# Attention's buffers handed to the experts' weights in seven parts instead of five, and one piece of output multiplied later

## The chip, the cores and the metric

The kernel runs on one core of one Trainium2 chip. The metric is the device time of one execution in microseconds (us). A core has five instruction streams that matter here: PE (TensorE, matrix products), DVE (VectorE), ACT (ScalarE), POOL (GpSimd) and SP (SyncE). SP computes nothing: it issues the transfers (DMA) between the device's memory and the on-chip memory, one after another, in the order of the program.

## The reference, cut to what matters

Attention over hashed buckets for 4 batches of 8 heads (768 positions, 64 wide), and behind it a soft mixture of 8 experts with 4 slots each.

```python
# attention, for each of the 32 (batch, head)
q_bucket = bits of (q @ proj > 0);  k_bucket likewise          # 6 bits
scores = where(q_bucket == k_bucket, (q @ k.T) / 8, -1e9)
out    = softmax(scores) @ v
x = out arranged as (3072 tokens, 512)
# soft mixture of experts
logits = x @ phi                                    # 32 slots
slot_input = softmax(logits, over tokens).T @ x     # 8 experts x 4 slots
slot_out[e] = relu(slot_input[e] @ w1[e]) @ w2[e]   # w1: 512x1024, w2: 1024x512, 8 experts
return softmax(logits, over slots) @ slot_out       # (3072, 512)
```

All numbers are 32-bit floats. The experts' weights are 32 MB and are read once.

## The kernel before, in words

**Attention.** The 32 heads run one behind another, two at a time in flight. For each head the kernel loads q and k, hashes and splits them, and puts them into one of three buffers `XY` (head h uses XY[h % 3]). PE then makes each head's scores twice: once for the maximum of each row (`smax`), and once for the exponentials (`scores`, line 711, which also needs one row of `XY` that is written late by a small transfer, `shift_rows`, line 576). ACT takes the exponentials into one of five buffers `pt` (line 717), POOL adds them up into one of three `acc` (lines 725 and 728), and PE multiplies them with v (`av`, line 737). v is loaded by `load_v` (line 558) into one of two buffers, head h into v[h % 2].

The order of the work is written out by hand: `at` (line 1050) takes each step with a time from the tables `WHEN`, `FIRST` and `LAST`, the steps are sorted by that time, and the loop that begins at line 1128 goes through whole-numbered slots and calls the steps of each slot in order. Six slots belong to a head, and `last` is slot 192, where the last head would begin to end. What a step emits goes to the queues of its engines in that order, so SP's queue has the loads and moves in the order in which the steps were called. SP waits at each transfer until the place that it writes is free and until the transfer eight before it in its own queue has landed, and everything behind it waits too.

**Weights.** The weights are cut into 64 pieces of 512 KB, tiles `w` of 128 x 1024, loaded in the order in which they will be used by `load_weights` (line 449) and `load_piece` (line 454; line 457 for w1, line 459 for w2). 22 pieces have buffers of their own (pool `wa`) and come in during attention, one every six slots. For the rest there is no room while attention runs. Attention's own buffers lie in pools on the other side of the memory, stacked upon one another, and are closed from the top as attention ends; pools of weights are opened in their place:

- slot `last` - 14: `pp` (raw q and k, their splits, the bits) becomes `wb`, 5 pieces, of which one is loaded in each of five slots
- slot `last` - 5: `yp` (two of the three `XY`) becomes `wy`, 6 pieces
- slot `last` - 2: `ap` (three of the five `pt`, two of the three `acc`, one of the two v) becomes `wp`, 6 pieces
- slot `last`: `lp` (one `pt`, one `XY`) becomes `wl`, 5 pieces
- slot `last` + 2: `mp` (the last `pt`, the last `acc`, the other v and small things) becomes `wc`, 1 piece

The other 19 pieces go into buffers that are used a second time: three into the last batch's tokens (`xq`), 16 into `wa`'s once their first pieces have been multiplied.

**Experts and output.** PE multiplies the slots with w1 (`hidden`, line 1191) and the result with w2 (`model`, line 1245), the second in two halves x of 256 columns each. `split_out` (line 1249) splits a half's result in two parts that are multiplied together later: ACT copies it (line 1251), DVE makes the rest (line 1252). `send` (line 1256) then makes the output of a half in six pieces: for each piece PE makes two products of two matmuls each (line 1266), DVE copies the one and ACT the other into a tile `w` of 512 KB (line 1268), and SP sends the tile out (line 1269). The tiles for sending, and one more, `halves`, for the split parts, come from `wy`'s six buffers. The end of the program is: the first half's `model`; `split_out`; 16 matmuls of the second half's `model`; `send` of the first half, six pieces; the other 48 matmuls of the second half's `model`; `split_out`; `send` of the second half, six pieces.

Of the kernel before, what the change touches and what calls it, by code (L numbers as in the profile page):

```python
# [9 lines left out]
F32 = mybir.dt.float32  # L10
F32R = mybir.dt.float32r
# [5 lines left out]
B, H, S, D, NB = 4, 8, 768, 64, 6  # L17
BH = B * H
P = 128
NT = S // P  # L20
# [3 lines left out]
E, SPE, F = 8, 4, 1024  # L24
# [8 lines left out]
N_R = 2 * NB + 1  # L33
N_Y = 3
N_P = 5
N_WA, N_WB, N_WY, N_WP, N_WL, N_WC = 22, 5, 6, 6, 5, 1


C_TH, C_AM, C_LO = 0, 1, 2
# [369 lines left out]
def held_pool(tc, name):  # L409
    stack = ExitStack()  # L410
    return stack.enter_context(tc.tile_pool(name=name, bufs=1, side="right")), stack.close
# [3 lines left out]
def lsh_attention_soft_moe(  # L415
# [15 lines left out]
    wa = ctx.enter_context(tc.tile_pool(name="wa", bufs=N_WA))  # L431
    dp = ctx.enter_context(tc.tile_pool(name="dp", bufs=1))

    mp, free_mp = held_pool(tc, "mp")
    lp, free_lp = held_pool(tc, "lp")
    ap, free_ap = held_pool(tc, "ap")
    yp, free_yp = held_pool(tc, "yp")
    pp, free_pp = held_pool(tc, "pp")


# [8 lines left out]
    def load_weights(pool, n):  # L449
        for _ in range(n):  # L450
            if len(wt) < len(pieces):
                load_piece(pool.tile([P, F], F32, name="w"))

    def load_piece(t):
        w, g, c, j = pieces[len(wt)]
        if w == 0:
            nc.sync.dma_start(out=t, in_=w1[4 * g + j, c * P:(c + 1) * P, :])
        else:
            nc.sync.dma_start(out=t, in_=w2[4 * (c // 2) + j, c % 2, g])
        wt[w, g, c, j] = t  # L460
# [8 lines left out]
        st[h]["raw"] = raw  # L469


    at_end = {(NT // 2 * BH - 1 - n) % N_P: held for n, held in enumerate((mp, lp) + (ap,) * (N_P - 2))}
    pts = [at_end[j].tile([P, 2 * S], F32, name=f"pt{j}") for j in range(N_P)]
    ones = cp.tile([P, 32], F32, name="ones")
    nc.vector.memset(ones, 1.0)
# [1 line left out]
    nc.vector.memset(idle, 1.0)  # L477
    mz_wide = mp.tile([P, 72], F32, name="mz")
    nc.vector.memset(mz_wide, 0.0)
    accs = [(mp if i == (BH - 1) % 3 else ap).tile([P, S], F32, name=f"acc{i}") for i in range(3)]  # L480
    vs = [held.tile([P, NT, D], F32, name=f"v{i}") for i, held in enumerate((ap, mp))]


# [49 lines left out]
    Ys, Xs = [], []  # L533
    XYs = []
    for i in range(N_Y):
        held = lp if i == (BH - 1) % N_Y else yp
        XYs.append(held.tile([P, 2, 2, S], F32R, name=f"XY{i}"))
        Xs.append(XYs[i][:, :, 0])
        Ys.append(XYs[i][:, :, 1])
# [508 lines left out]
    last = NT * BH  # L1048
# [19 lines left out]
    for h in range(BH):  # L1068
        s0, x = NT * h, h % 2
# [22 lines left out]
        if x and h < BH - 1:  # L1092
            p, p0 = h - 1, s0 - NT
# [34 lines left out]
    for slot in range(int(plan[0][0] // 1), last + 5):  # L1128
        if slot == last - 14:
            free_pp()  # L1130
            wb = ctx.enter_context(tc.tile_pool(name="wb", bufs=N_WB))
        if last - 14 <= slot < last - 14 + N_WB:
            load_weights(wb, 1)
        if slot == last - 5:
            free_yp()
            wy = ctx.enter_context(tc.tile_pool(name="wy", bufs=N_WY))
            load_weights(wy, N_WY)
        if slot == last - 2:
            free_ap()
            wp = ctx.enter_context(tc.tile_pool(name="wp", bufs=N_WP))  # L1140
            load_weights(wp, N_WP)
        if slot == last:
            free_lp()
            wl = ctx.enter_context(tc.tile_pool(name="wl", bufs=N_WL))
            load_weights(wl, N_WL)
        if slot == last + 2:
            free_mp()
            tp = ctx.enter_context(tc.tile_pool(name="tp", bufs=1))
            wc = ctx.enter_context(tc.tile_pool(name="wc", bufs=N_WC))
            fold = tp.tile([P, P], F32, name="fold")  # L1150
            nc.gpsimd.dma_start(out=fold, in_=cst[:, C_FD:C_ALL])
            load_weights(wc, N_WC)
            siT = tp.tile([P, KC, E, 32], F32, name="siT")
            nc.gpsimd.memset(siT, 0.0)
        while plan and plan[0][0] < slot + 1:
            f, *args = plan.pop(0)[2]
            f(*args)
# [57 lines left out]
    def more_weights(u):  # L1215
        turn_weights(cas[u], cts[B - 1][:, u * HC:(u + 1) * HC], q_a, "qa")
# [16 lines left out]
    hidden(hid[1], 1, range(1, KC))  # L1233
    hs1, hT1 = above_zero(hid[1])
    hTs = hT0, hT1
    for held, n in ((wa, N_WA - 18), (wb, N_WB), (wy, N_WY)):
        load_weights(held, n)


    halves = wy.tile([P, F], F32, name="w").bitcast(F32R).rearrange("p (n m) -> p n m", n=4)  # L1240

    def model(po, x, g, fs=range(FC)):
        for f in fs:
            for j in range(4):
                nc.tensor.matmul(po[32 * j:32 * j + 32], hTs[g][:, f, 32 * j:32 * j + 32],  # L1245
                                 wt[1, x, 2 * g + f // 4, j][:, (f % 4) * HM:(f % 4 + 1) * HM],
                                 start=(g + f == 0), stop=(g == 1 and f == FC - 1))

    def split_out(po, x):
        hi, so = halves[:, 2 * x], halves[:, 2 * x + 1]  # L1250
        nc.scalar.copy(hi, po)
        nc.vector.scalar_tensor_tensor(out=so, in0=hi, scalar=con[:, C_LO:C_LO + 1], in1=po,
                                       op0=ALU.mult, op1=ALU.add)
        return so

    def send(so, x):
        for n in range(B * NT // 4):
            ob = wy.tile([P, F], F32, name="w")
            for u in range(2):
                pool, name = ((q_h, "qh"), (q_h, "qh"), (q_a, "qa"))[(2 * n + u) % 3]  # L1260
                po = pool.tile([P, 512], F32, name=name)
                for t in range(2):

                    tt = 4 * n + 2 * u + t
                    bb, c, k = tt // NT, (tt % NT) // 3, tt % 3
                    nc.tensor.matmul(po[:, t * HM:(t + 1) * HM], cts[bb][:, (2 * k + c) * P:(2 * k + c + 1) * P], so,  # L1266
                                     start=True, stop=True)
                (nc.scalar.copy if u else nc.vector.tensor_copy)(ob[:, u * DM:(u + 1) * DM], po)
            nc.sync.dma_start(out=out[x, n], in_=ob)

    pos = [q_s.tile([P, 512], F32, name="qs")[:, 0:HM] for _ in range(2)]
# [4 lines left out]
    so0 = split_out(pos[0], 0)  # L1276
    more_weights(0)
    model(pos[1], 1, 0, range(4))
    more_weights(1)
    send(so0, 0)  # L1280
    model(pos[1], 1, 0, range(4, FC))
    model(pos[1], 1, 1)
    send(split_out(pos[1], 1), 1)


# [31 lines left out]
```

## Time and profile before

| | |
|---|---|
| median of three runs | 485.89 us (485.75 to 486.6) |
| the profiled execution's own time | 487.07 us |
| its span, from the first instruction to the last | 485.3 us |
| PE, DVE, ACT, POOL busy | 470.2, 356.9, 265.5, 335.2 us |
| moved by DMA | 93.66 MB, mean 193 GB/s |

All times of instructions are counted in us from the start of the span of one profiled execution. That execution took 1.2 us more than the median of the runs. A row of the timeline has the start, the length, the engine, the line of the kernel, the operation, the tile that is written and the tiles that are read, and how many equal instructions it merges; in brackets stands the idle time ahead of it and what ended that. A row of the windows has a stretch of time, its length, and then for each engine how long it was busy and with how many instructions; the last three columns are the clock that PE was granted (1.00 is full speed), the busy share of the 16 DMA engines, and GB/s. PE, DVE, ACT and POOL are shown by names; `PEld` is PE's loading of the matrix that stays, and `SPq` is the issue of a transfer by SP.

### The profile page before, as it was taken

What the parts mean: (1) busy time and instruction counts of PE and PEld (TensorE: products, weight loads), DVE (VectorE), ACT (ScalarE), POOL (GpSimd) and SP (SyncE); (2) the same over time, 40 slices, a digit from 0 to 9 for tenths busy, and PEclk for the clock granted to TensorE, in tenths of its full rate; (3) what the DMA queues carried; (4) which work ended last, traced back from release to release, by engine and by line L of the source; (5) the groups of instructions that cost most, each with busy time, mean ns of one, the idle gap of its engine ahead of it and who ended that gap; (6) DMA issues with size and microseconds to landing.
All of it is one profiled execution on the core that took longest, in us unless ns stands there. A gap on an engine that the chain in (4) does not pass through costs nothing.

```text
span 485.3 us, 8851 instructions
## 1 busy us (share of the span) xinstructions
PE 470.2 (97%) x3175; PEld 292.8 (60%) x3175; DVE 356.9 (74%) x666; ACT 265.5 (55%) x509; POOL 335.2 (69%) x206
## 2 busy tenths in 40 slices
PE   8899999999999999999999999999999999999992
PEld 6655756566666666666666575757566666663462
DVE  5557878888888888888888788888887882564133
ACT  4256656655566464747485565656656645423032
POOL 8385877777787887878797877777878778710000
PEclk9999999999999999999999999999999999999997
DMA  6745545747574746666565566676654266799997
GB/s 159 194 105 155 159 117 144 213 133 211 144 205 141 177 166 158 204 147 212 137 207 138 162 169 193 168 194 167 192 156 117 52 152 246 256 387 410 409 383 282
DMA packets 37455, 93.66 MB, mean 193 GB/s; under 512 B 7058, under 2 KB 13332, under 8 KB 37412
## 3 DMA queue, kind: packets, MB, share of 16 engines
q1 hardware_dynamic: 37280, 92.96, 64.5%
q8 instruction: 25, 0.41, 0.3%
q14 instruction: 18, 0.15, 0.1%
q10 hardware_dynamic: 100, 0.08, 0.1%
q0 software_dynamic: 32, 0.07, 0.0%
HBM read 52.76 MB, written 6.29 MB: 122 GB/s over the span
## 4 chain that ended last, share of the span: by engine, by line
PE 93%; DMA 2%; DVE 1%; SPq 0%; issue 0%; ACT 0%; DVEq 0%; ACTq 0%
PE st L711 28%; PE av L737 27%; PE smx L654 15%; PE qs L1245 3%; PE qh L1191 3%; PE mi L749 2%; PE mi L764 2%; PE mi L609 2%; PE mi L799 2%; DMA XY<-w 1%; PE mi L784 1%; PE av L528 1%; PE mi L958 1%; PE mi L696 1%; DMA raw<-qk 1%; PE qh L1266 1%
## 5 line engine op out<-in xcount | busy, mean ns | idle before, releaser
L728 POOL TENSOR_TENSOR acc<-acc,pt 128x768 f32<-128x768 f32 x125 | 245.1, 1971 | 34.1 <-ACT pt L717 28.3
L717 ACT ACTIVATE pt<-st 128x512 f32<-128x512 f32 x288 | 162.9, 594 | 56.0 <-PE st L711 52.5
L711 PE MATMUL st<-XY 128*128 128x512 f32 (+1 forms) x768 | 171.1, 343 | 0.0
L667 DVE TENSOR_REDUCE mx<-smx 128x1 f32<-128x512 f32 x192 | 128.7, 678 | 35.8 <-PE smx L654 32.6
L711 PEld LDWEIGHTS st<-XY 128*128 128x128 f32 x768 | 120.5, 189 | 24.8 <-issue 9.6
L737 PE MATMUL av<-pt,v 128*64 128x384 f32 x768 | 133.1, 491 | 0.0
L654 PE MATMUL smx<-XY 96*128 96x256 f32 (+1 forms) x384 | 119.9, 362 | 1.3 <-DVE mx L667 0.8
L737 PEld LDWEIGHTS av<-pt,v 128*64 128x64 f32 x768 | 51.4, 136 | 67.9 <-issue 65.0
L654 PEld LDWEIGHTS smx<-XY 96*128 96x128 f32 x384 | 68.2, 189 | 35.7 <-DVE mx L667 14.3
L725 POOL TENSOR_TENSOR acc<-pt 128x768 f32<-128x768 f32 x32 | 58.3, 1822 | 32.3 <-ACT pt L717 32.1
L664 DVE TENSOR_REDUCE mx<-smx 128x2 f32<-128x512 f32 x96 | 65.6, 685 | 10.8 <-PE smx L654 10.3
L741 ACT COPY avs<-av 128x384 f32<-128x384 f32 x32 | 15.3, 478 | 82.6 <-PE av L737 82.6
L572 DVE TENSOR_TENSOR w<-raw,w 128x768 fp32r<-128x768 f32 x28 | 41.8, 1494 | 0.0
L756 DVE RECIPROCAL sm<-sm 128x128 f32<-128x128 f32 x45 | 38.4, 910 | 0.0
L568 ACT CAST w<-raw 128x768 fp32r<-128x768 f32 x32 | 25.0, 830 | 4.6 <-DMA XY<-w 3.6
L801 DVE TENSOR_TENSOR xq<-mi,r 128x256 f32<-128x256 f32 x45 | 17.6, 418 | 9.6 <-PE mi L799 9.6
L585 ACT CAST XY<-w 64x768 fp32r<-64x768 f32 x30 | 23.4, 830 | 0.0
L602 DVE TENSOR_SCALAR bt<-mi,con 128x384 fp32r<-128x384 f32 x15 | 10.1, 676 | 13.4 <-PE mi L609 5.9
L609 PE MATMUL mi<-raw,pb 128*32 128x384 f32 x128 | 15.3, 498 | 2.0 <-DMA raw<-qk 1.9
L799 PE MATMUL mi<-ident,avs 128*128 128x128 f32 x90 | 14.7, 272 | 0.0
L1245 PE MATMUL qs<-w 128*32 128x256 f32 x232 | 14.6, 380 | 0.0
L572 POOL TENSOR_TENSOR w<-raw,w 128x768 fp32r<-128x768 f32 x4 | 7.2, 1819 | 10.7 <-ACT w L568 9.4
(181 smaller groups left out, 327.2 us busy)
## 6 DMA issues: line engine op xcount, KB each, us to landing
w<-w SPq DMA_DIRECT2D x61, 512.0 KB
XY<-w SPq DMA_DIRECT2D x48, 384.0 KB
raw<-qk SPq DMA_DIRECT2D x32, 384.0 KB
XY<-w SPq DMA_DIRECT2D x64, 192.0 KB
v<-vt SPq DMA_DIRECT2D x32, 192.0 KB
out<-w SPq DMA_DIRECT2D x12, 512.0 KB
xq<-w SPq DMA_DIRECT2D x3, 512.0 KB
XY<-bt SPq DMA_DIRECT2D x60, 19.5 KB
```

The costliest lines, as they stand in the source:

```text
L572: (nc.vector if h > 2 else nc.gpsimd).tensor_tensor(out=w[:, 2 * x + 1], in0=st[h]["raw"][:, x], in1=w[:, 2 * x], op=ALU.subtract)
L609: nc.tensor.matmul(pts_b[j // 2 if h == 0 else 0][32 * j:32 * j + 32, 0:HC], pb[:, 32 * (j // 2):32 * (j // 2) + 32], st[h]["raw"][:, j // ...
L654: nc.tensor.matmul(pt[:, o:o + b - a], s["Y"][0:96, 0, t * P:(t + 1) * P], s["Y"][0:96, 1, a:b], start=True, stop=True)
L664: nc.vector.tensor_reduce(out=mx[:, n - 1:n + 1], in_=s["sm_ps", n - 1].rearrange("p (a x) -> p a x", a=2), axis=AX.X, op=ALU.max)
L667: nc.vector.reduce_max(out=mx[:, n:n + 1], in_=s["sm_ps", n], axis=AX.X)
L711: nc.tensor.matmul(pt[:, o:o + b - a], x[:, 1, i * P:(i + 1) * P], x[:, 0, a:b], start=first, stop=not first)
L717: nc.scalar.activation(s["P", n // 4][:, 512 * u:512 * u + 512], s["st_ps", n - (n % 4 == 2)], AF.Exp, scale=D ** -0.5)
L725: nc.gpsimd.tensor_tensor(out=s["acc"], in0=pr[:, 0:S], in1=pr[:, S:2 * S], op=ALU.add)
L728: eng.tensor_tensor(out=s["acc"], in0=s["acc"], in1=pr[:, a * S:(a + 1) * S], op=ALU.add)
L737: nc.tensor.matmul(s["av"][64 * c:64 * c + 64, 0:HC], s["v"][:, i, :], pr[:, o + c * HC:o + (c + 1) * HC], start=(i == 0), stop=(i == NT - 1))
L756: nc.vector.reciprocal(out=rs[:, k * P:(k + 1) * P], in_=rs[:, k * P:(k + 1) * P])
L1245: nc.tensor.matmul(po[32 * j:32 * j + 32], hTs[g][:, f, 32 * j:32 * j + 32], wt[1, x, 2 * g + f // 4, j][:, (f % 4) * HM:(f % 4 + 1) * HM] ...
```

## The change

Attention's pools are cut finer, in seven instead of five, and closed in other slots:

- slot `last` - 14: `pp` becomes `wb`, 5 pieces, and in the same slot a new pool `xp` (the `XY` of the last head but two) becomes `wx`, 3 pieces. All eight are loaded in this slot, one behind another.
- slot `last` - 6: `yp` (now one `XY`, that of the last head but one) becomes `wy`, 3 pieces
- slot `last` - 4: `ap` (now two `pt`, one `acc`, one v) becomes `wp`, 4 pieces
- slot `last` - 2: `lp` (now one `XY`, one `acc`) becomes `wl`, 4 pieces
- slot `last`: a new pool `lq` (two `pt`) becomes `wq`, 3 pieces
- slot `last` + 2: `mp` becomes `wc`, 1 piece, as before

The pieces, their order and the transfers are the same 64. The tiles for sending now come from `wb`'s five buffers, and `halves` from `wx`. At the end of the program the sixth piece of the first half's output is made behind the second half's `model` and `split_out` instead of ahead of them.

```diff
-N_WA, N_WB, N_WY, N_WP, N_WL, N_WC = 22, 5, 6, 6, 5, 1
+N_WA, N_WB, N_WX, N_WY, N_WP, N_WL, N_WQ, N_WC = 22, 5, 3, 3, 4, 4, 3, 1
...
     mp, free_mp = held_pool(tc, "mp")
+    lq, free_lq = held_pool(tc, "lq")
     lp, free_lp = held_pool(tc, "lp")
     ap, free_ap = held_pool(tc, "ap")
     yp, free_yp = held_pool(tc, "yp")
+    xp, free_xp = held_pool(tc, "xp")
     pp, free_pp = held_pool(tc, "pp")
...
-    at_end = {(NT // 2 * BH - 1 - n) % N_P: held for n, held in enumerate((mp, lp) + (ap,) * (N_P - 2))}
+    at_end = {(NT // 2 * BH - 1 - n) % N_P: held for n, held in enumerate((mp, lq, lq) + (ap,) * (N_P - 3))}
...
-    accs = [(mp if i == (BH - 1) % 3 else ap).tile([P, S], F32, name=f"acc{i}") for i in range(3)]
+    accs = [(mp if i == (BH - 1) % 3 else lp if i == (BH - 2) % 3 else ap).tile([P, S], F32, name=f"acc{i}") for i in range(3)]
...
-        held = lp if i == (BH - 1) % N_Y else yp
+        held = lp if i == (BH - 1) % N_Y else yp if i == (BH - 2) % N_Y else xp
...
         if slot == last - 14:
             free_pp()
             wb = ctx.enter_context(tc.tile_pool(name="wb", bufs=N_WB))
-        if last - 14 <= slot < last - 14 + N_WB:
-            load_weights(wb, 1)
-        if slot == last - 5:
+            load_weights(wb, N_WB)
+            free_xp()
+            wx = ctx.enter_context(tc.tile_pool(name="wx", bufs=N_WX))
+            load_weights(wx, N_WX)
+        if slot == last - 6:
             free_yp()
...
-        if slot == last - 2:
+        if slot == last - 4:
             free_ap()
...
-        if slot == last:
+        if slot == last - 2:
             free_lp()
             wl = ctx.enter_context(tc.tile_pool(name="wl", bufs=N_WL))
             load_weights(wl, N_WL)
+        if slot == last:
+            free_lq()
+            wq = ctx.enter_context(tc.tile_pool(name="wq", bufs=N_WQ))
+            load_weights(wq, N_WQ)
...
-    for held, n in ((wa, N_WA - 18), (wb, N_WB), (wy, N_WY)):
-        load_weights(held, n)
-
-
-    halves = wy.tile([P, F], F32, name="w").bitcast(F32R).rearrange("p (n m) -> p n m", n=4)
+    load_weights(wa, N_WA - 16)
+
+
+    halves = wx.tile([P, F], F32, name="w").bitcast(F32R).rearrange("p (n m) -> p n m", n=4)
...
-    def send(so, x):
-        for n in range(B * NT // 4):
-            ob = wy.tile([P, F], F32, name="w")
+    def send(so, x, ns):
+        for n in ns:
+            ob = wb.tile([P, F], F32, name="w")
...
-    send(so0, 0)
+    send(so0, 0, range(5))
     model(pos[1], 1, 0, range(4, FC))
     model(pos[1], 1, 1)
-    send(split_out(pos[1], 1), 1)
+    so1 = split_out(pos[1], 1)
+    send(so0, 0, range(5, 6))
+    send(so1, 1, range(6))
```

In the order of the instructions this moves rows at two places. The first is SP's queue about the slot `last` - 14. `XY<-mr` is the late row of a head's `XY`, `w<-w` is a piece of the weights, and `v<-vt` a head's v: of the two, the first is for the last head but one and the second for the last head. Before:

```order
L576 DMA XY_141<-mr 1x12x128
L457 DMA w<-w 128x1024 x3
L558 DMA v_94<-vt 128x384
L457 DMA w<-w 128x1024 x2
L558 DMA v_95<-vt 128x384
L576 DMA XY_142<-mr 1x12x128
L457 DMA w<-w 128x1024 x5
```

Now:

```order
L578 DMA XY_147<-mr 1x12x128
L459 DMA w<-w 128x1024 x8
L560 DMA v_100<-vt 128x384
L560 DMA v_101<-vt 128x384
L578 DMA XY_148<-mr 1x12x128
L459 DMA w<-w 128x1024 x2
L461 DMA w<-w 128x1024 x13
```

Eight pieces of weights, instead of three and five, now stand ahead of the two v, and the last head's late row stands behind all of them, as before.

The second place is the end of PE's queue. `qh<-w` and `qa<-w` are the products for the output (two rows of two matmuls, or one, to a piece), `qs<-w` with 48 matmuls is the rest of the second half's `model`. Before:

```order
L1266 MATMUL qh<-w,ct_120 128x256 x4
L1266 MATMUL qa<-w,ct_120 128x256 x2
L1266 MATMUL qh<-w 128x256 x4
L1266 MATMUL qa<-w 128x256 x2
L1245 MATMUL qs<-w 32x256 x48
L1266 MATMUL qh<-w,ct_118 128x256 x4
L1266 MATMUL qa<-w,ct_118 128x256 x2
```

Now:

```order
L1273 MATMUL qh<-w,ct_126 128x256 x4
L1273 MATMUL qa<-w,ct_126 128x256 x2
L1273 MATMUL qh<-w 128x256 x2
L1252 MATMUL qs<-w 32x256 x48
L1273 MATMUL qh<-w 128x256 x2
L1273 MATMUL qa<-w 128x256 x2
L1273 MATMUL qh<-w,ct_124 128x256 x4
```

Four matmuls, the sixth piece of the first half, moved from ahead of the 48 to behind them. On DVE and on ACT the copies of that piece moved in the same way: they now stand behind the split of the second half (lines 1251 and 1252 before) and ahead of the second half's own copies. The rest of PE's, DVE's, ACT's and POOL's queues is in the same order as before.

## The prediction

> **What bounds the kernel now.** I read the profile's page first, for the engine that carries the chain, and the sizes of the transfers.
>
> ```profile
> span 485.3 us, 8851 instructions
> PE 470.2 (97%) x3175; PEld 292.8 (60%) x3175; DVE 356.9 (74%) x666; ACT 265.5 (55%) x509; POOL 335.2 (69%) x206
> PE 93%; DMA 2%; DVE 1%; SPq 0%; issue 0%; ACT 0%; DVEq 0%; ACTq 0%
> w<-w SPq DMA_DIRECT2D x61, 512.0 KB
> v<-vt SPq DMA_DIRECT2D x32, 192.0 KB
> ```
>
> The second row is busy time, the third the chain that ended last: 93% of the span is PE following upon PE. So a microsecond in which PE stands still is a microsecond of the result, unless it falls where PE waits already. The change moves transfers and, at the end, four matmuls. So I ask two things of the trace: does PE wait for weights anywhere (then earlier loads help), and does PE wait, or come near to waiting, for anything that the loads now overtake. The waits of PE from 436 us on, where the experts run, have one row:
>
> ```profile
> PE qh L1266 <- DVE w L1252: 1.0, 1, 1.0
> ```
>
> PE waits there once, 1.0 us, for the second half's split, and for no weights. Loading them earlier is worth nothing to PE: I cost this part at 0, and the cover is that nothing of PE's stands still for a piece. For the other question I took SP's timeline from the slot `last` - 14 on, PE's a little later, and the traffic in windows.
>
> ```profile
> 398.86 2.09 SPq L457 DMA_DIRECT2D w<-w  x3
> 401.05 0.37 SPq L558 DMA_DIRECT2D v<-vt  x1
> 401.47 0.91 SPq L457 DMA_DIRECT2D w<-w  x2
> 403.47 0.33 SPq L558 DMA_DIRECT2D v<-vt  x1
> 410.11 0.81 SPq L576 DMA_DIRECT2D XY<-mr  x1
> ```
>
> ```profile
> 399.34 4.09 PE L737 MATMUL av<-pt,v 128*64 128x384 f32 x24
> ...
> 409.50 0.85 PE L749 MATMUL mi<-acc,ones 128*32 128x384 f32 x8
> 410.28 2.80 PE L737 MATMUL av<-pt,v 128*64 128x384 f32 x16
> 413.01 0.55 PE L784 MATMUL mi<-ident,sm 128*128 128x128 f32 x3
> 413.32 1.42 PE L711 MATMUL st<-XY 128*128 128x256 f32 x6
> ...
> 422.12 2.16 PE L737 MATMUL av<-pt,v 128*64 128x384 f32 x12
> ```
>
> ```profile
> 400.00:408.00 8.00, 8.00 (x49) 5.41 (x46) 2.94 (x6) 4.06 (x8) 7.11 (x4) 1.00 0.95 361
> 408.00:410.00 2.00, 2.00 (x20) 1.29 (x18) 0.94 (x4) 1.72 (x5) 1.70 (x1) 1.00 0.12 43
> 440.00:450.00 10.00, 10.00 (x96) 3.48 (x92) 3.96 (x12) 2.80 (x12) 1.02 (x4) 1.00 1.03 409
> ```
>
> The 16 matmuls at 410.28 are the first to read the v that was issued at 401.05, that of the last head but one. PE follows without a break before and behind them, so today this v has landed by then. The DMA engines work at full share from 400 to 408 and are empty at 408.2 (0.12 of the 2 us). Five pieces and two v, 5 x 512 + 2 x 192 KB = 3.01 MB, went through in that time.
>
> **Part 1, eight pieces ahead of the two v.** The loads that the change puts ahead may be issued as soon as before: the first five need what they needed, and the place of the next three is the `XY` of the last head but two, whose scores PE has finished when it begins that head's `av` at 399.34, before SP's sixth issue. Whether transfers of one queue pass each other decides the rest. In the saturated stretch SP's own waits tell:
>
> ```profile
> SPq L459 <- DMA w<-w: 8.7, 11, 0.9
> 443.97 0.33 SPq L459 DMA_DIRECT2D w<-w  x1
> 445.24 0.33 SPq L459 DMA_DIRECT2D w<-w  x1
> ```
>
> Each issue there waits for the transfer eight before it to land, and the issues are 1.27 us apart: 512 KB at 409 GB/s take 1.28 us. Landings come one by one at the pace of one piece, not in a bunch, so I take the queue as first in, first out, and v as behind all eight pieces.
>
> Three pieces more are 1.573 MB. At the 361 GB/s of this stretch they take 4.36 us, at the 409 GB/s of the saturated one 3.85 us. So the queue is empty at 408.2 + 4.36 = 412.6 (or 412.05). The last head's v is behind the one that matters, 0.197 MB or 0.5 us, so the wanted v has its last byte at 412.1 (or 411.55). From the last byte until PE goes on there is a receipt. It isn't below 0; from above, one row bounds it: the sixth piece's copy waits for the first output's transfer, issued at 465.08, to leave its tile.
>
> ```profile
> 465.08 0.35 SPq L1269 DMA_DIRECT2D out<-w  x1
> 468.33 0.59 ACT L1268 COPY w<-qa 128x512 f32<-128x512 f32 x1 [1.33 <-DMA out<-w]
> ```
>
> That is 3.25 us from issue to release, of which 1.28 us is the transfer, so start and receipt together are at most 2.0 us. I take 0.5 us, as the start has a share in it and the queue was not empty at 465. PE then goes on at 412.6 instead of 410.28: **a stall of 2.3 us**. The ends are 1.3 us (fast rate, no receipt) and 3.8 us (slow rate, 2.0 us). By the Trainium skill, DMA: Bandwidth & Descriptors, section Anatomy of one DMA, a transfer has about 2.0 us of fixed cost, most of it the receipt behind the last byte; by that the stall would be 3.8 us and the time 489.7. The row above agrees only with a sum of 2.0 us for both sides, so I stay with 0.5.
>
> What is late next: the last head's row `XY<-mr` is issued at 410.11 as now, since PE's transpose and ACT's copy for it stand ahead of the stall. It lands behind both v, about 413, and the scores at 413.32 that need it have moved to 415.6. The last head's v is wanted at 422. Neither adds. SP's remaining loads wait for places that attention frees 2.3 us later, with 0 for PE as above. Nothing later gives the 2.3 us back: behind the stall the chain is PE upon PE again.
>
> **Part 2, the sixth piece behind the second half's model.**
>
> ```profile
> 465.91 0.76 PE L1266 MATMUL qh<-w 128*128 128x256 f32 x4
> 466.51 0.40 PE L1266 MATMUL qa<-w 128*128 128x256 f32 x2
> 466.84 5.39 PE L1245 MATMUL qs<-w 128*32 128x256 f32 x96
> 472.29 0.37 ACT L1251 CAST w<-qs 128x256 fp32r<-128x256 f32 x1 [3.37 <-PE qs L1245]
> 472.70 0.48 DVE L1252 SCALAR_TENSOR_TENSOR w<-w,con,qs 128x256 fp32r<-128x256 f32 x1 [3.65 <-ACT w L1251]
> 473.23 0.73 PE L1266 MATMUL qh<-w,ct 128*128 128x256 f32 x4 [1.01 <-DVE w L1252]
> 473.77 0.69 DVE L1268 COPY w<-qh 128x512 f32<-128x512 f32 x1 [0.59 <-PE qh L1266]
> 474.05 1.07 ACT L1268 COPY w<-qh 128x512 f32<-128x512 f32 x2 [1.38 <-PE qh L1266]
> 474.66 0.33 SPq L1269 DMA_DIRECT2D out<-w  x1
> ```
>
> Six matmuls take 465.91 to 466.84, 0.93 us, and four of them go: the model starts and ends 0.62 us earlier, the split ends at 472.56 instead of 473.18, and the four run in the 1.01 us in which PE waits for it. So PE gains 0.62 us. But what ends the program is the output's transfers:
>
> ```profile
> 474.00:476.00 2.00, 2.00 (x18) 1.94 (x17) 2.00 (x4) 1.96 (x4) 0.00 (x0) 1.00 0.33 129
> 476.00:477.00 1.00, 0.45 (x4) 0.24 (x3) 1.00 (x3) 1.00 (x3) 0.00 (x0) 1.00 0.98 389
> 478.00:479.00 1.00, 0.00 (x0) 0.00 (x0) 0.00 (x0) 0.00 (x0) 0.00 (x0) 0.67 1.04 414
> 482.00:484.00 2.00, 0.00 (x0) 0.00 (x0) 0.00 (x0) 0.00 (x0) 0.00 (x0) 0.50 0.65 258
> ```
>
> From about 475.35 (0.33 of the first row's 2 us) to 483.3 (0.65 of the last row's) the DMA engines are full with the second half's six pieces, 7.95 us or 1.33 us each, while PE is done before 477. With the change the first of this train is the sixth piece of the first half: DVE copies it behind the split, 472.56 to 473.3, and SP issues it at about 473.33 instead of 474.66, 1.33 us earlier. But seven transfers follow and not six, 1.33 us more (1.28 by the pace of the loads): **0**. The second half's first piece is copied from 473.3 on, its transfer is due one transfer later, and so the engines keep ahead. The ends are -0.62 us (if the transfers did not set the pace) and +0.69 us (if DVE's added copy, 0.69 us, came to stand on the path).
>
> **The sum.** Span 485.3 + 2.3 + 0 = 487.6 us. The profiled execution took 487.07, its span and 1.8 us around it; the median of the runs is 485.89, 1.2 us less. The difference goes on the median: 485.89 + 2.3 = **488.2 us**.
>
> **Rivals.**
>
> *A stall that also costs the clock.* After its last matmul, which ends about 476.45 (0.45 of the row 476 to 477), PE's granted clock is still 1.00, and it falls to half at 478.34 (0.67 in the row 478 to 479 is a third at 1.00 and the rest at 0.50). So 1.9 us without a matmul were enough there; the 1.01 us before the split were not, as the clock stayed at 1.00. A stall of 2.3 us lies above both. If the clock falls, PE runs at half speed for some time. If it comes back as fast as it went, in 1.9 us, that costs 0.95 us: 489.2 us. It decides from a stall of about 1.9 us on, and on how the stall lies to whatever the clock is measured by, which no row shows. By the Trainium skill, TensorE: Matmul & The Clock Gate, Part 1, the clock falls after an idle window of about 3.4 us, and the windows run free; by that rule a stall of 2.3 us would leave the clock alone and the time stays 488.2. The trace's 1.9 us speak against the rule as it stands, so this rival keeps a large chance. By the same page it takes about 3.4 us of work to come back, which would cost 1.7 us and give 489.9.
>
> *v lands in time.* Then only part 2 is left and nothing is changed: 485.9 us. For it: transfers of one queue run on 16 engines, and I saw their order only through equal pieces. Against: 8 pieces and one v, 4.39 MB, would have to pass between 400 and about 409.8, 448 GB/s, above any row (414), so v would have to overtake the pieces. That the last byte decides, as said, is in the code: PE's first `av` waits for the whole tile.
>
> *Faster.* No stall, and the end of the program closes the hole in the traffic: from 474 to 476 the DMA engines stand still for 0.67 x 2 = 1.3 us. If the sixth piece's transfer began just where the first five end, the whole hole would go: 484.6 us. It decides at an issue of the sixth piece before 472; the copies behind the split put it at 473.3, and the stall of part 1 would have to be missing too.
>
> **How the numbers follow.** A measurement of this kernel can tell about 0.2% from no change, 0.97 us. Stall with the clock kept, 488.2: 0.51. Stall with the clock halved, 489.2 to 489.9: 0.34. v in time, 485.9: 0.10. Faster, 484.6: 0.05. So slower 0.85, same 0.10, faster 0.05. The likeliest gives 488.2. For the range, 1.3 us of stall give 487.2, less 0.3 for a gain at the end, 486.9; at the other end the stall with the clock at 489.9 and 0.7 for a later receipt or the end's loss, 490.6. The first two cases fill it but for their tails; left out are the last two.
>
> **What would show it.** Right: in the profile of the changed kernel the first `av` of the last head but one waits for the transfer of v, 1.3 to 3.8 us, at about 410.3; the windows show full traffic from 400 to 412 and no hole at 408 to 412; every later row of PE is later by that much; the last issue of an output is later by that too. The granted clock just behind the stall tells the first two cases apart. Wrong: if that `av` starts at 410.3 as before, the queue does not keep its order, and the whole of part 1 falls. If the span grows by less than the stall, something behind it had slack that I did not find. If the issues of the output shift by more or less than the stall, part 2 is mis-sized.

## The result and the profile after

| | before | changed |
|---|---|---|
| median of six runs each, side by side | 486.25 us (485.75 to 487.08) | 492.04 us (489.3 to 492.43) |
| ratio, 95% interval | | 1.0083 [1.0056, 1.011] |
| the profiled execution's time, its span | 487.07, 485.3 us | 489.3, 487.5 us |

The change makes the kernel slower. The ratio on 486.25 us is 490.3 us, while the medians lie further apart, 5.8 us. The six runs of the changed kernel fall into two groups, and their median lies in the upper one: 489.3 and 489.85 us at a mean granted clock of 0.995, and 492.04 to 492.43 us at 0.986 to 0.991. (The mean takes in the end of the program, where PE is done and its clock falls.) The profiled execution is of the first group. Two runs of the experiments below, 590 us in the first and 1607 us in the ninth, were disturbed: the ratios leave them out, the medians count them.

From the page of the changed kernel: the span, the chain that ended last, and the costliest group.

```profile
span 487.5 us, 8851 instructions
PE 89%; DMA 5%; SPq 2%; ACT 1%; DVE 1%; issue 1%; DVEq 0%; ACTq 0%
L739 PE MATMUL av<-pt,v 128*64 128x384 f32 x768 | 133.1, 491 | 2.6 <-DMA v<-vt 2.6
```

In the last row the number behind the second bar is idle time of PE ahead of these matmuls: 2.6 us in all, all of it put down to v's transfer. SP's timeline and PE's, at the places that the prediction showed of before:

```profile
398.54 5.14 SPq L459 DMA_DIRECT2D w<-w  x8
403.72 1.60 SPq L560 DMA_DIRECT2D v<-vt  x2
409.82 0.81 SPq L578 DMA_DIRECT2D XY<-mr  x1
```

```profile
409.20 0.85 PE L751 MATMUL mi<-acc,ones 128*32 128x384 f32 x8
412.61 2.80 PE L739 MATMUL av<-pt,v 128*64 128x384 f32 x16 [2.55 <-DMA v<-vt]
415.34 0.55 PE L786 MATMUL mi<-ident,sm 128*128 128x128 f32 x3
415.64 1.40 PE L713 MATMUL st<-XY 128*128 128x256 f32 x6
```

Eight pieces are issued in a row, then both v. The `av` that followed its forerunner without a break in before now waits 2.55 us for its v and begins at 412.61; the prediction had 412.6. The scores behind it come 2.32 us later than in before (415.64 against 413.32). The windows, with the granted clock, the DMA engines' share and GB/s in the last columns:

```profile
408.00:410.00 2.00, 2.00 (x17) 1.00 (x16) 0.64 (x4) 1.58 (x4) 1.92 (x2) 1.00 1.02 418
410.00:412.00 2.00, 0.05 (x4) 0.00 (x0) 0.00 (x0) 1.07 (x2) 1.92 (x2) 1.00 0.97 377
412.00:414.00 2.00, 1.40 (x10) 0.68 (x12) 0.00 (x0) 0.00 (x0) 1.92 (x2) 1.00 0.97 324
414.00:416.00 2.00, 2.00 (x16) 1.04 (x13) 0.08 (x1) 0.00 (x0) 1.92 (x2) 1.00 1.01 387
```

The hole in the traffic (0.12 of 408 to 410 before) is gone. PE stands still (it is busy for 0.05 of the 2 us from 410 to 412), and in this execution its clock stays at 1.00. At the end, SP's issues of the last outputs, in before and in the changed kernel:

```profile
474.66 5.36 SPq L1269 DMA_DIRECT2D out<-w  x6
475.56 6.62 SPq L1276 DMA_DIRECT2D out<-w  x7
```

Seven in a train, as forecast, ending at 482.18 (475.56 + 6.62) where before's six ended at 480.02: 2.16 us later, and the span is 2.2 us longer.

A figure that leaves the start of a run out serves for the comparisons below: the time from the eight `mi<-acc,ones` matmuls just ahead of the place of the stall (409.20 here) to the end of the span, called **the rest**. It is 75.8 us in before (485.3 - 409.50) and 78.3 us here.

### The profile page after: what moved, and what is told of

The parts are those of the page before. It is cut to its first block, busy times and chain, and to the rows that moved or that the text cites. A ratio compares the mean times of both kernels' runs of the same rounds, so it can differ in the third digit from the quotient of the medians.

```text
span 487.5 us, 8851 instructions
## 1 busy us (share of the span) xinstructions
PE 471.3 (97%) x3175; PEld 293.0 (60%) x3175; DVE 357.3 (73%) x666; ACT 265.8 (55%) x509; POOL 335.5 (69%) x206
## 4 chain that ended last, share of the span: by engine, by line
PE 89%; DMA 5%; SPq 2%; ACT 1%; DVE 1%; issue 1%; DVEq 0%; ACTq 0%
PE st L713 27%; PE av L739 25%; PE smx L656 15%; PE qs L1252 3%; PE qh L1199 3%; PE mi L766 2%; PE mi L611 2%; PE mi L751 2%; PE mi L801 2%; DMA v<-vt 2%; DMA XY<-w 1%; PE mi L786 1%; SPq L459 1%; PE av L530 1%; PE mi L960 1%; PE mi L698 1%
```

## The experiments

The theory: the loads that were put ahead delay v by their own transfer time, and the stall is that. The rivals: the end of the program costs something too, or the stall's main price is the clock that it takes along. The diffs are against the changed kernel, where nothing else is said. All kernels compute the whole result; in the fourth and fifth PE multiplies something more that nothing reads.

**v ahead of the pieces.** One line in the table `LAST`:

```
+ ('load_v', -2): -14.005,
```

> The changed kernel, with one number more in the table of times: the load of the last head but one's v is issued ahead of the eight pieces of weights instead of behind them. Everything else of the change stays. If the loss is v's place in SP's queue, the first av of that head waits for nothing, the two groups of runs (489.3 to 489.9 and 492.0 to 492.4) become one, and the time is that of the kernel before, 485.3 to 486.6 us, ratio 0.999 to 1.001. If the handing over costs by itself (the earlier traffic, the new places in memory, the end of the program), 2 us or more of the loss stay.

Measured: 488.36 us against 487.19, ratio 1.0019 [1.0001, 1.0036]; the rest is 76.7 us. PE's waits and its timeline:

```profile
PE st L714 <- DMA XY<-mr: 0.6, 1, 0.6
```

```profile
412.40 2.80 PE L740 MATMUL av<-pt,v 128*64 128x384 f32 x16
416.31 0.97 PE L714 MATMUL st<-XY 128*128 128x256 f32 x4 [0.63 <-DMA XY<-mr]
```

The wait for v is gone, and with it most of the loss, though not all: the ratio lies above the 0.999 to 1.001 that were expected. PE now waits 0.6 us at the last head's scores for its late row of `XY`, a transfer of 6 KB that still stands behind the eight pieces. In the changed kernel the stall for v had covered this one.

**The end alone.** The kernel before, with only the end of the program changed:

```
-    def send(so, x):
-        for n in range(B * NT // 4):
+    def send(so, x, ns):
+        for n in ns:
...
-    send(so0, 0)
+    send(so0, 0, range(5))
...
-    send(split_out(pos[1], 1), 1)
+    so1 = split_out(pos[1], 1)
+    send(so0, 0, range(5, 6))
+    send(so1, 1, range(6))
```

> The kernel before, with only the last part of the change: the sixth piece of the first half's output behind the second half's model and split. Theory: PE gains 0.6 us and the train of output transfers is longer by one, 0 in all, within 0.3 us, ratio 0.9994 to 1.0006. Rivals: the transfers don't set the pace, 0.6 us faster (0.9988); or the added copies stand on the path, 0.7 us slower (1.0014).

Measured: 487.22 us against 487.19, ratio 0.9998 [0.9981, 1.0015]; the rest is 75.65 us. SP's timeline:

```profile
473.27 6.60 SPq L1269 DMA_DIRECT2D out<-w  x7
```

The sixth piece is issued at 473.27 (the prediction computed 473.33), and the last issue ends at 479.87, 0.15 us ahead of before's. So this part gives about 0.15 us in the profiles, which the runs cannot tell from zero.

**One piece fewer ahead of v.**

```
-            load_weights(wx, N_WX)
+            load_weights(wx, N_WX - 1)
+        if slot == last - 8:
+            load_weights(wx, 1)
```

> The changed kernel, with the eighth piece of weights loaded behind the two v instead of ahead of them. If v waits for each piece ahead of it, it lands one piece earlier: the wait at the first av falls from 2.55 us by 1.28 to about 1.3 us. A wait of 1.3 us should be too short for the clock to fall however it lies, so all runs should lie together, 1.0 to 1.4 us over the kernel before, ratio 1.002 to 1.003. If the spread of the changed kernel has another cause than the clock, runs 2.5 us above the others stay.

Measured: 489.05 us against 487.19, ratio 1.0035 [1.0017, 1.0054]; the rest is 78.0 us. PE's waits:

```profile
PE av L739 <- DMA v<-vt: 2.1, 1, 2.1
```

The direction is right, the size is not: 0.45 us less wait than with eight pieces, where a piece is 1.28 us, and 1.86 us over before where 1.0 to 1.4 were expected. Nor do all runs lie together: two of twelve, at 489.86 and 491.99 us, have a mean clock of 0.991 and 0.989. The trace records each of the 16 DMA engines' shares of a transfer apart. v's median share lands at 411.31 here, but the slowest at 412.56, 1.25 us later, and PE needs them all. In the changed kernel's first profile the slowest was 0.5 us behind the median at 412.05, in the sixth experiment's 1.7 us. Counted from the eight `ones` matmuls (409.64 here, 409.20 there), the median share came 1.67 us behind them instead of 2.85: 1.18 us earlier, close to one piece. The slowest share took most of that back.

**PE kept busy while it waits.** In the place of the stall PE multiplies the identity by itself:

```
+    def fill(n):
+        pt = p_av.tile([P, 512], F32, name="av")
+        for _ in range(n):
+            nc.tensor.matmul(pt[:, 0:P], ident, ident, start=True, stop=True)
...
+    at(last - 6.4, fill, 22)
```

> The changed kernel, with 22 matmuls of the identity with itself, whose product nothing reads, ahead of the last head but one's av, so that PE works through the wait for v. The wait stays, the idle time goes. If the runs at 492 us are those in which the granted clock fell behind the wait, all runs now lie with the lower group, 2.2 to 2.8 us over the kernel before, ratio 1.0045 to 1.0058. If the upper group has another cause, it stays and the ratio stays at 1.008.

Measured: 493.14 us against 487.19, ratio 1.0117 [1.0094, 1.0139]. PE's timeline:

```profile
411.83 5.18 PE L536 MATMUL av<-ident 128*128 128x128 f32 x44
```

The filling was sized wrongly: a product is two instructions, so the 22 took 5.18 us, twice the stall, and the time says nothing of the price of the clock. Of the clock itself the runs say something: it is 0.993 to 0.996 in all six, where the changed kernel had four of six at 0.991 or less.

**The same with a filling of the right size**, `at(last - 6.4, fill, 10)`:

> The changed kernel, with 10 matmuls of the identity with itself ahead of the last head but one's av, their product read by nothing. Each is two instructions of about 0.12 us, so they take 2.4 us and end within the wait for v of 2.0 to 2.6 us, where 22 of them had taken 5.2 us. If part of the changed kernel's loss is the clock that falls behind the wait, no run has a mean granted clock under 0.992 and the median is 2.0 to 2.8 us over the kernel before, ratio 1.004 to 1.006, under that of the changed kernel in this call. If the clock has no part, both have the same time and the same share of runs under 0.992.

Measured: 490.97 us (489.45 to 491.81) against 487.79, ratio 1.0062 [1.0039, 1.0086]; the rest is 78.7 us. PE's timeline:

```profile
409.77 2.50 PE L536 MATMUL av<-ident 128*128 128x128 f32 x20
412.72 2.80 PE L745 MATMUL av<-pt,v 128*64 128x384 f32 x16 [0.46 <-DMA v<-vt]
```

2.50 us of filling and 0.46 us of waiting take the place of the stall, 2.96 us in all. One run of six is at a clock under 0.992, where none was expected, and the ratio lies a little above the expected range. The interval also overlaps with the changed kernel's of the same call (the next run), so the times do not show that the filling saves anything.

**The changed kernel again**, unedited, beside the last one:

> The changed kernel itself, for more runs with their clocks and a second profile, beside the others of this call. With a wait of 2.0 to 2.6 us and a clock that falls in some runs: median 2.5 to 4.5 us over the kernel before, ratio 1.005 to 1.009, about half of the runs under 0.992 in the mean clock and those 1.5 us or more above the others. If the clock has no part, the runs lie in one group 2.0 to 2.6 us over.

Measured: 491.75 us (488.93 to 494.69) against 487.79, ratio 1.0088 [1.0057, 1.012]. Five of nine runs have a clock under 0.992, with a median of 493.95 us; the other four have a median of 489.84. None of the 26 runs of before beside it is under 0.992. This time the profiled execution is one of those with the lower clock, and the rest is 82.7 us. PE's waits, its timeline, and the windows:

```profile
PE av L739 <- DMA v<-vt: 4.0, 1, 4.0
```

```profile
409.92 0.85 PE L751 MATMUL mi<-acc,ones 128*32 128x384 f32 x8
414.80 5.39 PE L739 MATMUL av<-pt,v 128*64 128x384 f32 x16 [4.03 <-DMA v<-vt]
420.12 0.75 PE L786 MATMUL mi<-ident,sm 128*128 128x128 f32 x3
420.63 1.41 PE L713 MATMUL st<-XY 128*128 128x256 f32 x6
```

```profile
412.00:414.00 2.00, 0.00 (x0) 0.00 (x0) 0.00 (x0) 0.00 (x0) 1.92 (x2) 0.94 1.04 385
414.00:416.00 2.00, 1.20 (x4) 0.53 (x6) 0.00 (x0) 0.00 (x0) 1.92 (x2) 0.50 1.04 417
416.00:418.00 2.00, 2.00 (x8) 0.71 (x6) 0.00 (x0) 0.00 (x0) 1.92 (x2) 0.50 0.48 184
418.00:420.00 2.00, 2.00 (x8) 0.48 (x4) 0.00 (x0) 0.00 (x0) 0.08 (x1) 0.50 0.04 16
420.00:422.00 2.00, 2.00 (x13) 1.43 (x11) 1.05 (x3) 0.00 (x0) 0.00 (x0) 0.85 0.00 0
```

The clock is halved from about 413.8 (0.94 of the first row) to 420.6 (0.85 of the last). The trace's own clock records have 413.77 and 420.59, 6.83 us. The 16 matmuls at 414.80 take 5.39 us, where the first profile has 2.80. From the `ones` matmuls to the scores it is 10.71 us (420.63 - 409.92) against 6.44 (415.64 - 409.20): 4.27 us more, 1.47 of them a longer wait and 2.80 the clock. The longer wait is mostly one DMA engine: 15 of v's 16 shares had landed by 413.14, the last one came at 414.76.

**The three pieces after the late row.** v first as in the first experiment, and `xp` closed later:

```
+ ('load_v', -2): -14.005,
...
             load_weights(wb, N_WB)
+        if slot == last - 6:
             free_xp()
             wx = ctx.enter_context(tc.tile_pool(name="wx", bufs=N_WX))
             load_weights(wx, N_WX)
-        if slot == last - 6:
             free_yp()
```

> The changed kernel with the last head but one's v ahead of the first five pieces, and the other three pieces loaded in slot last - 6, behind the last head's late row, with the pool that follows. Theory: neither v nor the late row then waits behind more than before, PE waits for neither, and the time is that of the kernel before, within 0.5 us, ratio 0.999 to 1.001, below the kernel in which v alone was put ahead (1.0019), in which PE waited 0.6 us for the late row. If earlier traffic or the new places cost by themselves, 1 us or more stays.

Measured: 486.68 us against 487.79, ratio 0.9994 [0.997, 1.0017]; the rest is 75.65 us. SP's timeline and PE's:

```profile
397.48 3.88 SPq L460 DMA_DIRECT2D w<-w  x5
401.74 0.33 SPq L561 DMA_DIRECT2D v<-vt  x1
408.37 0.81 SPq L579 DMA_DIRECT2D XY<-mr  x1
409.23 2.54 SPq L460 DMA_DIRECT2D w<-w  x5
```

```profile
407.75 0.85 PE L752 MATMUL mi<-acc,ones 128*32 128x384 f32 x8
408.54 2.80 PE L740 MATMUL av<-pt,v 128*64 128x384 f32 x16
```

PE goes from one row to the next without a wait, and the loss is gone, though the memory is still cut into the change's seven parts. A repetition (the ninth run) is the same:

> The version with v ahead of five pieces and three pieces behind the late row, once more, since its median was below that of the kernel before (0.9994) and the interval, 0.997 to 1.0017, settled nothing. The theory has no gain in it: no wait of PE before went away, and the end of the program gave 0. So 0.999 to 1.001 again. Rival: finer parts are worth something by themselves, 0.5 us or more, ratio 0.998 to 0.999.

Measured: 487.15 us against 487.33, ratio 0.9986 [0.9963, 1.001], the rest 75.7 us. The ratio lies in the range of the rival, a gain of 0.5 us from finer parts, but the interval holds both answers, and the rest is the 75.8 us of before to within 0.1. With the first half's sixth piece back in its old place, `send(so0, 0, range(6))`:

> The same, with the sixth piece of the first half's output back in its place ahead of the second half's model, so that only the seven parts are left of the change. Theory: the same time as with it, ratio to the kernel before 0.999 to 1.001; the last output issued within 0.3 us of where it is issued with the change at the end. Rival: the move at the end gains 0.6 us here, ratio 1.001 over that of the version with it.

Measured: 486.75 us against 487.33, ratio 0.9997 [0.9975, 1.002], the rest 75.8 us. No version is shown to be faster than before: each of these three intervals holds 1. The order at the end is worth 0.15 us in the profiles, as in the second experiment.

**v and the late row by another queue.** ACT issues the two transfers, in the old places:

```
-        nc.sync.dma_start(out=st[h]["v"], in_=vt[h])
+        (nc.scalar if h == BH - 2 else nc.sync).dma_start(out=st[h]["v"], in_=vt[h])
...
-        move(s["XY"][ROW:ROW + 1, 0].rearrange("o y (t p) -> o (y t) p", p=P), mr)
+        move(s["XY"][ROW:ROW + 1, 0].rearrange("o y (t p) -> o (y t) p", p=P), mr, nc.scalar if h == BH - 1 else nc.sync)
```

> The changed kernel, with the last head but one's v and the last head's late row issued by ACT instead of SP; the eight pieces stay where they are. If a transfer waits for what is ahead of it in its own queue alone, and the DMA engines serve both queues in turn, v is issued at about 404.5, has landed by 408, PE waits for neither, and the time is that of the kernel before plus at most 0.5 us, ratio 0.999 to 1.0015. If the engines work through all that is issued in the order of issue, v lands at 412.5 again and the wait stays, ratio 1.005 or more.

Measured: 488.55 us against 487.79, ratio 1.0016 [0.9993, 1.0039]; the rest is 76.6 us. The timelines of SP, of ACT and of PE:

```profile
399.20 6.59 SPq L459 DMA_DIRECT2D w<-w  x8
```

```profile
404.62 0.39 ACTq L560 DMA_DIRECT2D v<-vt  x1
```

```profile
411.55 2.80 PE L739 MATMUL av<-pt,v 128*64 128x384 f32 x16 [0.86 <-DMA v<-vt]
```

This lies between the two forecasts. PE still waits 0.86 us for v. By the transfers' records v's first packet moved at 408.11, 3.5 us after the issue, and its shares landed from 410.2 to 411.5, ahead of the eighth piece's (median 412.2): on the other queue v got a share of the engines, but did not go ahead of all the pieces. That the two queues share is what the Trainium skill, DMA: Bandwidth & Descriptors, section Queues, rings and completion order, says: each DMA engine goes round the queues that have work for it, a packet at a time. The trace agrees that v passed part of the pieces; why 192 KB still took 5.6 to 6.9 us beside them is open.

The rest, in the order of its length:

| kernel | PE's wait for a transfer, us | the rest, us |
|---|---|---|
| end alone; three later; three later again | 0 | 75.65; 75.65; 75.7 |
| before; three later with the old end | 0 | 75.8; 75.8 |
| v by ACT's queue | 0.86 | 76.6 |
| v first | 0.63 | 76.7 |
| seven ahead | 2.10 | 78.0 |
| changed | 2.55 | 78.3 |
| short filling | 2.96, of it 2.50 filled | 78.7 |
| long filling | 5.24, of it 5.18 filled | 81.65 |
| changed, clock halved | 4.03 | 82.7 |

The second column holds the filling too. All rows but the last two follow it to within 0.4 us (over 75.7 us). The long filling has 0.7 us beyond it, and PE's waits there have one that the other profiles have not:

```profile
PE mi L1188 <- ACT fold L999: 0.7, 1, 0.7
```

The last has 3.0 us beyond its wait.

## Why the prediction was right, and where it was not

**Part 1, the mechanism: right.** The eight pieces stand ahead of v in one queue, v lands behind them, and the `av` of the last head but one waits, at the forecast place (412.61 against 412.6) and by about the forecast amount (2.55 us against 2.3). Putting v first takes the wait away, and with the three pieces moved behind the late row as well the loss is gone (0.9994 and 0.9986). The rivals in which v lands in time are refuted. That the place agrees to 0.01 us is luck: PE's rows just ahead were 0.30 us earlier in this execution than in before (409.20 against 409.50), and in the sixth experiment's profile the same `av` began at 414.80.

**The stall as one number: too narrow.** Its range of 1.3 to 3.8 us came from rate and receipt. The profiles of one and the same kernel have 2.55 and 4.03 us, the upper one beyond the range. The step "I take 0.5 us" for the receipt was about right: in the sixth experiment's profile the slowest engine's last packet of v ended at 414.38, and its signal, for which PE waits, came at 414.76, 0.38 us later. The 2.0 us that the prediction quotes from the Trainium skill stand there for transfers that GpSimd issues; SP's loads here do not show them behind the last byte. What the sum lacked is a term for the spread of the engines: it let the queue be empty at one time ("the queue is empty at 408.2 + 4.36 = 412.6"), but the wait ends with the slowest of 16, which was 0.5 to 1.7 us behind the median share. Why the lag changes from run to run is open.

**"It lands behind both v, about 413 … Neither adds": right only under the stall.** With v first, PE waits 0.63 us for the late row. It too stood behind the eight pieces, and the stall for v had hidden its price.

**Weights earlier, 0: right.** With all else repaired, the earlier loads of the change give nothing that the runs show.

**Part 2, 0: right.** The sixth piece is issued at 473.27 against the computed 473.33, seven transfers follow where there were six, and the end gains about 0.15 us in the profiles.

**The clock: the failed step.** The likeliest case, the stall with the clock kept at 488.2 us, is what the first profile shows, and two of six runs and four of nine. The other nine of fifteen have a mean clock under 0.992, where the rival had a chance of 0.34. The step of this rival that failed is its price: "If it comes back as fast as it went, in 1.9 us, that costs 0.95 us". In the one profile that shows it, the clock was halved for 6.83 us and cost 2.80 us. By that, a run with the lower clock is at 488.2 + 2.8 = 491.0 us or above, and the median of six that holds four such is 492.04, above the range's 490.6; the ratio's 490.3 is in it. That is partly luck: the range's upper end added 1.7 us for the clock and 0.7 us for a late receipt or the end of the program, and what the profile shows is 2.8 us for the clock and nothing lost at the end. Filling the wait with products supports the clock's part from the other side: none of six runs and one of six were under 0.992. That the lower clock in the other eight runs comes from the same place is inferred from their mean clock and time, since only one of them has a profile. Not every such run need come from the stall: in the versions in which PE waits for no transfer (the end alone, three later twice, three later with the old end) 4 of 47 runs are under 0.992 too, and the profiled run of v first, at 0.991, lost its clock at 25.6 us.

By the Trainium skill, TensorE: Matmul & The Clock Gate, Part 1, a halved clock follows on an idle window of about 3.4 us, and about 3.4 us of work bring it back; the prediction used that for 489.9 us. The measured 6.83 us are two such windows, of 3.41 us each. The fall came 3.0 us after PE's last matmul, before a whole window had gone by, so on this point the trace and the page differ.

Open beyond this: runs with a clock of 0.992 and more still spread from 486 to 489.6 us in before, and nothing here says why.

## What to carry to other kernels

When bulk loads are moved ahead in a queue that keeps its order, look for every small transfer that now stands behind them, and for the time at which its reader wants it: not the first alone, since the next is covered by the first one's stall. Issue the small ones ahead, and the bulk behind them. Price a stall of PE with what its clock may lose behind it, for a whole period or two, and not with the wait alone.

## What the runs showed of the hardware that was not expected

The length of a wait does not decide alone whether the clock falls. It fell 1.9 us after PE's last matmul at the end of before, and was kept through waits of 2.55 us (changed) and 2.10 us (seven ahead). Early in the program, where PE also waits for loads in before, the kernel with v first shows:

```profile
22.00:24.00 2.00, 1.20 (x8) 0.14 (x4) 0.00 (x0) 0.00 (x0) 0.00 (x0) 1.00 0.51 111
24.00:26.00 2.00, 1.22 (x5) 0.70 (x4) 1.73 (x3) 0.70 (x1) 0.00 (x0) 0.91 0.04 13
26.00:28.00 2.00, 2.00 (x9) 1.81 (x9) 1.12 (x3) 1.46 (x3) 1.79 (x2) 0.50 0.08 20
28.00:30.00 2.00, 2.00 (x12) 1.67 (x13) 0.40 (x1) 0.44 (x1) 2.00 (x3) 0.74 0.15 38
```

PE is idle for 0.80 + 0.78 = 1.58 us of the first two rows, in pieces, and by these rows the clock is halved from 25.64 to 29.04, 3.4 us (3.41 in the trace's clock records). In before PE is idle there for 1.73 us, and the windows have 1.00 throughout:

```profile
22.00:24.00 2.00, 1.05 (x5) 0.43 (x6) 0.10 (x1) 0.00 (x0) 0.00 (x0) 1.00 0.38 91
24.00:26.00 2.00, 1.22 (x7) 0.75 (x7) 2.00 (x4) 1.56 (x2) 0.65 (x1) 1.00 0.01 4
```

Two lengths of halved clock, 3.41 and 6.83 us, are one and two of the same period, and in the trace's clock records the changes of one execution lie whole multiples of 3.41 us apart (with v first 20.48, 3.41 and 453.97 us: 6, 1 and 133 of them). That fits a clock which is judged once per period, on the idle time within it, with the program's place in the period left to chance. It would explain why one kernel's runs make two groups, and why the two waits cost differently: with v first PE had no idle time in the period after the fall, and the clock came back at its end; in the sixth experiment the wait reached 1.03 us into that period, and the clock came back one period later. Its threshold is an estimate: laid on that grid, the idle time in the period ahead of a fall was 1.58 us (v first), 1.90 (the end of before) and 2.99 (sixth experiment), and 1.59 (seven ahead) and 1.63 us (changed) in periods after which the clock was kept. So it lies near 1.6 us, a little under half a period; the values overlap, and the record does not fix it more closely.
